# Filter results of the spectral layer stored to memory unit by unit and read back with classes on partitions

## The chip, the cores and the metric

The kernel runs on one core of a Trainium2 chip. A core has a matrix engine (TensorE; its matmuls are PE, its weight loads PEld), a vector engine (DVE), a scalar engine (ACT), GpSimd (POOL) and a queue engine for transfers (SP). They run in parallel, each through its own instructions in order, and wait for each other by semaphores; 16 DMA engines move data between memory and the on-chip buffer of 128 partitions. PSUM, the matmuls' output memory, has eight banks of 512 f32 a partition. The metric is device time in microseconds of the whole program, the median of several runs.

## The reference

Two attention layers and two spectral layers alternate on one sequence of 2048 rows and 1024 columns, f32. In the spectral layer the normalised rows go through a two-dimensional real FFT, are multiplied by a complex filter and come back:

```
def _B_ref(x, w_r, w_i):
    X = jnp.fft.rfft2(x, axes=(-2, -1))
    X = X * (w_r + 1j * w_i)
    return jnp.fft.irfft2(X, s=(S, D), axes=(-2, -1))

x = x + _A_ref(_layernorm(x), A_wqkv, A_wo)
x = x + _B_ref(_layernorm(x), B_w_r, B_w_i)
x = x + _A_ref(_layernorm(x), A_wqkv, A_wo)
x = x + _B_ref(_layernorm(x), B_w_r, B_w_i)
```

## The kernel before

`attention()` and `spectral()` run once for each of two layers. Two buffers of 128 x 16384 f32 hold a whole sequence each: `big` and `R`. `spectral()` has three parts.

*First part.* The transform over one factor of the columns: transposes (`t1`, L1017) and matmuls (`fa`, L1032) put the data into `big`, laid out by g (2 halves), class c (128), q (64).

*Unit loop.* The 256 classes are handled in 32 units (16 of g = 0, then 16 of g = 1), 30 of four frequencies and two of five. `fb(i)` and `fc(i-1)` are the forward matmuls (L1099, L1131), DVE and POOL multiply by the filter `w` (L1138 to L1150; `w` loaded by SP in `loadw`, L1066, 256 KB a unit, two units ahead), `binv(i-3)` and `cinv(i-4)` are the inverse (L1099, L1171). `cinv` ends in an ACT copy (L1177) from PSUM into `big`, in the place of the unit's input. Every second unit SP loads 512 KB of y, the attention result, into `R` (16 loads).

*Last stage.* The inverse over the columns needs the classes on partitions, and in `big` they lie along the row. For each i of 16 and each g, `t2` transposes four 128 x 128 f32 blocks on TensorE (L1207) and ACT copies them to `tt` (L1209). `ai` multiplies them with the constant `mi` (L1219, f32, two passes each), and the results of the two halves are added to y: ACT copies the first (`e`, L1228), DVE takes the difference (L1229) and adds both to the left half of the columns (L1230, L1231), POOL adds the difference to the right half, for two i at a time (L1236; L1233 for i = 14); i = 15 is done on DVE alone (L1242). The transposes of i stand ahead of the matmuls of i - 1.

In layer 0 the last stage also prepares weights of layer 1's attention: `prep` loads staging tiles `wst` (L302), ACT scales them to f16 (L215) and DVE takes the rest (L216), in turns with the stage's work (`next(nxt)`); DVE starts the statistics of the next norm (L1255, six tiles). Behind it `tile_root` and L158 (DVE), L122 (POOL), L365 (ACT), L371 (PE) begin the next layer. In layer 1 the last stage stores the output: seven stores of 1 MB on SP (L1261), in pieces of 512 bytes, and the last 1 MB in two halves on SP and ACT (L1259).

A scheduler sets the order of each engine's instructions; only the last DVE additions are in an order written out by hand. SP issues its transfers in order, and one that waits holds back all behind it.

## Time and profile before

| | us |
|---|---|
| median of 3 runs (lowest, highest) | 3699.69 (3699.19, 3700.08) |
| the profiled execution | 3698.24 |
| its span, first to last instruction | 3696.4 |
| busy in it: PE, DVE, ACT, POOL | 3638.1, 3132.0, 2935.4, 666.2 |
| layer 0: last inverse matmul starts; last stage's last matmul group starts | 1799.74; 1845.21 |
| layer 0: next layer's first statistics (L158) start | 1850.03 |
| layer 1: last inverse matmul starts; last stage's last matmul group starts | 3636.64; 3681.53 |
| mean granted clock of TensorE | 0.997 |

The page sums up busy times over the whole span. A window row gives busy time and count for PE, PEld, DVE, ACT and POOL, then the granted clock, the mean busy share of the 16 DMA engines and GB/s. A timeline row is start, duration, engine, line, operation, output<-input and shape; in brackets the idle time before it and what ended it. A group row gives busy time and mean duration in ns. A transfer row gives size and median time from issue to landing.

### The profile page before, as it was taken

Reading aid. Unit: us, or ns where it says so; the run is one execution under the profiler, and the core shown is the slowest. Engines: PE = TensorE matmul, PEld = TensorE weight load, DVE = VectorE, ACT = ScalarE, POOL = GpSimd, SP = SyncE. Lnnn points to the kernel's source line nnn. Section 1 sums busy time; section 2 is a strip of 40 time slices with the busy share of each in tenths; the row PEclk is TensorE's granted clock in tenths of the full one; section 3 lists DMA queues with packets and bytes.
Section 4 is the critical chain, followed back from the end, with each engine's and each line's share of the span. In section 5 each row is a group of like instructions: output and inputs, shape, how many; then the busy total and the mean of one; then the engine's idle time right before and its main releaser. Section 6 shows DMA issues by size and latency. Waiting matters only on the chain.

```text
span 3696.4 us, 80677 instructions
## 1 busy us (share of the span) xinstructions
PE 3638.1 (98%) x32919; PEld 1628.6 (44%) x32919; DVE 3132.0 (85%) x3800; ACT 2935.4 (79%) x3653; POOL 666.2 (18%) x798
## 2 busy tenths in 40 slices
PE   8999999999999999999999999999999999999998
PEld 5333433343343333378953334333433433333888
DVE  7799899989998989876768898999899889788754
ACT  5788888888888967758747888888888889676686
POOL 1022112211221110014410111111111111100244
PEclk9999999999999999999999999999999999999999
DMA  6122222222232442143151232323222334321423
GB/s 197 21 53 53 52 53 53 58 47 56 47 63 50 99 112 77 70 155 97 56 165 21 56 58 50 56 49 62 42 53 53 63 57 98 101 78 74 171 84 109
DMA packets 203614, 274.33 MB, mean 74 GB/s; under 512 B 75872, under 2 KB 122592, under 8 KB 202208
## 3 DMA queue, kind: packets, MB, share of 16 engines
q1 hardware_dynamic: 164272, 195.06, 16.6%
q0 software_dynamic: 37632, 73.43, 13.8%
q8 instruction: 260, 4.26, 0.5%
q14 instruction: 122, 1.00, 0.1%
q10 hardware_dynamic: 1328, 0.59, 0.1%
HBM read 149.00 MB, written 118.42 MB: 72 GB/s over the span
## 4 chain that ended last, share of the span: by engine, by line


## 5 line engine op out<-in xcount | busy, mean ns | idle before, releaser
L724 ACT ACTIVATE p<-s,bias 128x1024 f32<-128x1024 f32 x2048 | 2171.0, 1112 | 457.5 <-PE s L720 439.5
L743 DVE TENSOR_TENSOR R<-R,p 128x1024 f32<-128x1024 f32 x896 | 1044.7, 1220 | 69.9 <-ACT p L724 67.6
L743 DVE TENSOR_TENSOR acc<-acc,p 128x1024 f32<-128x1024 f32 x896 | 1044.1, 1220 | 55.9 <-ACT p L724 54.9
L730 PE MATMUL o<-p,R 128*32 128x512 f32 x8192 | 985.0, 598 | 0.0
L411 PE MATMUL x<-big,wqk 128*128 128x512 f16 x2880 | 676.4, 380 | 3.2 <-ACT R L473 1.9
L720 PEld LDWEIGHTS <-R 32*128 32x128 f16 x12288 | 229.4, 92 | 740.5 <-issue 624.8
L411 PEld LDWEIGHTS <-wqk 128*128 128x128 f16 x3072 | 275.8, 98 | 418.8 <-issue 127.6
L730 PEld LDWEIGHTS o<-p,R 128*32 128x32 f32 x8192 | 213.7, 109 | 523.4 <-issue 523.4
L720 PE MATMUL s<-Q,R 32*128 32x512 f16 x6144 | 425.4, 378 | 1.9 <-DVE mqk L445 1.9
L720 PE MATMUL s<-R 32*128 32x512 f16 x6144 | 426.3, 377 | 0.2
L469 PE MATMUL x<-wv,big 128*128 128x256 f16 x2784 | 330.5, 275 | 4.1 <-DVE R L216 2.2
L469 PEld LDWEIGHTS <-big 128*128 128x128 f16 x3072 | 291.0, 98 | 96.6 <-issue 55.9
L532 PE MATMUL x<-big 128*128 128x512 f16 x1008 | 231.9, 380 | 0.0
L749 POOL DMA_DIRECT2D zd<-R x112 | 93.4, 834 | 670.3 <-DMA zd<-R 282.2
L749 POOL DMA_DIRECT2D zd<-acc x112 | 92.5, 826 | 656.4 <-DVE z L759 306.8
L532 PEld LDWEIGHTS <-big 128*128 128x128 f16 x1428 | 134.3, 98 | 164.7 <-issue 28.4
L741 DVE SCALAR_TENSOR_TENSOR R<-p 128x1024 f32<-128x1024 f32 x64 | 75.5, 1222 | 97.3 <-ACT p L724 97.3
L752 POOL DMA_DIRECT2D zd<-zd x112 | 89.5, 799 | 367.3 <-DMA zd<-zd 154.8
L1150 DVE TENSOR_TENSOR H<-G,H 128x512 f16<-128x512 f32 (+1 forms) x68 | 47.4, 697 | 98.7 <-ACT H L1149 98.6
L741 DVE SCALAR_TENSOR_TENSOR acc<-p 128x1024 f32<-128x1024 f32 x64 | 75.8, 1221 | 45.1 <-ACT p L724 45.1
L1092 ACT COPY U<-ps 64x256 f32<-64x256 f32 (+1 forms) x272 | 97.2, 357 | 7.9 <-PE ps L1099 2.6
L1099 PE MATMUL ps<-cbi,H 128*128 128x256 f16 (+1 forms) x792 | 99.0, 273 | 3.5 <-DVE H L1150 2.2
(459 smaller groups left out, 3322.9 us busy)
## 6 DMA issues: line engine op xcount, KB each, us to landing
zd<-R POOLq DMA_DIRECT2D x112, 256.0 KB, 4.1
zd<-acc POOLq DMA_DIRECT2D x112, 256.0 KB, 4.1
wst<-in_wp SPq DMA_DIRECT2D x96, 256.0 KB, 3.4
R<-y SPq DMA_DIRECT2D x32, 512.0 KB, 6.0
w<-in_w SPq DMA_DIRECT2D x60, 256.0 KB, 2.7
zt<-zr SPq DMA_DIRECT2D x224, 64.0 KB, 2.7
od<-ohl SPq DMA_DIRECT2D x56, 256.0 KB, 2.4
big<-od SPq DMA_DIRECT2D x12, 896.0 KB, 6.4
```

Source lines behind the costliest of these rows:

```text
L411: nc.tensor.matmul(ps, a, b, start=i == 0, stop=i == 23)
L469: nc.tensor.matmul(ps[:, j], x[c][:, d, o:o + 128], w[:, n, d], start=i == 0, stop=i == 23)
L532: nc.tensor.matmul(p, a, b, start=start and d == ds[0] and i == 0, stop=stop and d == ds[-1] and i == 2)
L720: nc.tensor.matmul(s[h // 2][:, h % 2], K[g][r, a, kt * 128:kt * 128 + 128], Q[g][r, b, c * 512:c * 512 + 512], start=i == 0, stop=i == 2)
L724: nc.scalar.activation(p, s[hf], AF.Exp, bias=bias[g], scale=SCALE / (SQ * SQ))
L730: nc.tensor.matmul(O[g, c][32 * h:32 * h + 32], V[g][:, kt, 32 * h:32 * h + 32], P[g, c, kt, h // 2][:, h % 2], start=kt == 0, stop=kt == ...
L741: last_add = nc.vector.scalar_tensor_tensor(a, P[g, c, 0, hf], 1e-34, p, op0=ALU.add, op1=ALU.add)
L743: last_add = nc.vector.tensor_add(a, a, p)
L749: nc.gpsimd.dma_start(z, a[32 * j:32 * j + 32].rearrange("p a j n -> p (a j n)"), max_dma_last_dim=2048, **({"accum_op": ALU.add} if j els ...
L752: nc.gpsimd.dma_start(z[0:n], z[n:2 * n], accum_op=ALU.add, max_dma_last_dim=2048)
L1092: nc.scalar.copy(ov[64 * r:64 * r + 64, a0:a0 + m, x], tl[64 * x:64 * x + 64, :m, r])
L1099: nc.tensor.matmul(out, l, r, start=k == 0, stop=k == len(mm_) - 1)
```

## The change

`cinv` copies its result to a small tile `T` (three buffers) instead of `big`, and SP stores it to a table `zt` in memory: 256 KB a unit, 1024 pieces of 256 bytes. `turn(i)` reads the unit back in one transfer into eight partitions, 32 KB each, so that classes come to lie on partitions (`turned`, in `R`). The row order of the constant `mi` follows (`row`), and `mi` is loaded once, in layer 0. y is now loaded into `big`, behind the units whose input has been used, over the whole loop; after each spectral layer `big` and `R` swap names (`swap`).

The last stage has no transposes and no `tt`. A half step `ai(a, g)` is eight matmuls whose stationary operand is read from `turned` with a stride of 256 bytes, into one of four PSUM tiles of two banks. `even(a)` takes g = 0: ACT copies to `e` (128x1024), DVE adds; `odd(a)` takes g = 1: DVE subtracts and adds, POOL adds to the right half. Evens 0 to 3 run first. a = 7 is half as before and half on DVE. In layer 0 four of the weight tiles (k0 and q0 parts of the first phase's `wqk`) are scaled and cast on ACT (L321, L322) and subtracted on POOL (L323) instead of DVE.

```diff
+def row(i, s):
+    return 32 * (i % 16 // 4) + 4 * s + i % 4
...
         for i, (h, l, _) in enumerate(sl):
-            split(nc, h, l, st[i], SW)
+            if self.flag is None and ph in PH0[1:]:
+                nc.scalar.activation(st[i], st[i], AF.Copy, scale=SW)
+                nc.scalar.copy(h, st[i])
+                nc.gpsimd.tensor_tensor(l, st[i], h, op=ALU.subtract)
+            else:
+                split(nc, h, l, st[i], SW)
             load()
...
-        t_ = bu[:, g, i % 16]
+        t_ = p3.tile([128, 8, 64], F32, name="T")
         if n == 4:
             nc.scalar.copy(t_.rearrange("p (r j) q -> p j r q", j=4), pt)
         else:
             for o, v in ((0, pt[:, 0:3, 0]), (5, pt[:, 0:3, 1]), (3, pt[:, 3])):
                 nc.scalar.copy(t_[:, o:o + v.shape[1]], v)
+        nc.sync.dma_start(zt[i].rearrange("s p q -> p s q"), t_)
+
+    def turn(i):
+        g, r0 = UNITS[i][0], row(i, 0)
+        nc.sync.dma_start(turned[r0:r0 + 29:4, g], zt[i])
...
+        if 0 <= i - 5 < 32:
+            turn(i - 5)
         if 0 <= i - 4 < 32:
             cinv(i - 4)
...
         if i % 2 and i < 32:
             t = i // 2
-            nc.sync.dma_start(ap.x[:, t], yd[t * 128:(t + 1) * 128, :])
+            nc.sync.dma_start(rest[:, t], yd[t * 128:(t + 1) * 128, :])
+    turn(31)
...
+    ap.swap()
...
+    def ai(a, g):
+        p = pq.tile([128, 8, 128], F32, name="ai")
+        for q in range(8):
+            nc.tensor.matmul(p[:, q], turned[:, g, :, 8 * a + q], cst["mi"][:, g], start=True, stop=True)
+        return p.rearrange("p q (t u) -> p t u q", u=8)
+
+    def even(a):
+        p = ai(a, 0)
+        e = ap.pp.tile([128, 8, 128], F32, name="e", tag="p")
+        ev = e.rearrange("p q (t u) -> p t u q", u=8)
+        x0 = xo[:, 0, a]
+        h = 8 if a < 7 else 4
+        nc.scalar.copy(e[:, :h], p.rearrange("p t u q -> p q (t u)")[:, :h])
+        nc.vector.tensor_add(x0[:, :, :, :h], x0[:, :, :, :h], p[:, :, :, :h])
+        return p, e, ev
+
+    def odd(a, p0, e, ev):
+        p = ai(a, 1)
+        x0, x1 = xo[:, 0, a], xo[:, 1, a]
+        h = 8 if a < 7 else 4
+        nc.vector.tensor_sub(e[:, :h], e[:, :h], p.rearrange("p t u q -> p q (t u)")[:, :h])
+        nc.vector.tensor_add(x0[:, :, :, :h], x0[:, :, :, :h], p[:, :, :, :h])
+        nc.gpsimd.tensor_tensor(x1[:, :, :, :h], x1[:, :, :, :h], ev[:, :, :, :h], op=ALU.add)
...
+    first = [even(a) for a in range(4)]
+    for a in range(8):
+        odd(a, *first.pop(0))
+        if a < 4:
+            first.append(even(a + 4))
```

TensorE, from the last inverse matmuls of layer 0 (L1171) into its last stage. Before:

```order
L1171 MATMUL ps<-ci,U 128x128 x3
L1207 MATMUL ps<-ident,big 128x128 x14
L1219 MATMUL ps<-mi,tt 128x128 x8
L1207 MATMUL ps<-ident,big 128x128 x8
L1219 MATMUL ps<-mi,tt 128x128 x8
```

After (the lines have moved: L1192 is the inverse matmul; each `ai` tile is one half step, in the order even 0 to 3, odd 0, even 4, odd 1, even 5):

```order
L1192 MATMUL ps_21611<-ci_18686,U_21596 128x128 x4
L1238 MATMUL ai_21665<-mi_66,R_93 128x128 x8
L1238 MATMUL ai_21677<-mi_66,R_93 128x128 x8
L1238 MATMUL ai_21689<-mi_66,R_93 128x128 x8
L1238 MATMUL ai_21701<-mi_66,R_93 128x128 x8
L1238 MATMUL ai_21713<-mi_66,R_93 128x128 x8
L1238 MATMUL ai_21725<-mi_66,R_93 128x128 x8
L1238 MATMUL ai_21748<-mi_66,R_93 128x128 x8
L1238 MATMUL ai_21760<-mi_66,R_93 128x128 x8
```

The transposes are gone, and the matmuls read the buffer that the turns fill.

SP at the end of layer 0's loop, where before only filter loads, the constant and then staging loads stood. After (`zt<-T` is the store of a unit, L1206 the turns; the three of L1202 ahead of the last turns are units 28 to 30):

```order
L1206 DMA R<-zt 8x8192 [waits DMAHW7_49,DMAHW4_49]
L1202 DMA zt<-T 128x8x64 [waits DMAHW0_49,Activation_49]
L1202 DMA zt<-T 128x8x64 [waits DMAHW1_49,Activation_49]
L1202 DMA zt<-T 128x8x64 [waits DMAHW2_49,Activation_49]
L1206 DMA R<-zt 8x8192 [waits DMAHW0_49,DMASW1_49]
L1206 DMA R<-zt 8x8192 [waits DMAHW1_49]
L1206 DMA R<-zt 8x8192 [waits DMAHW5_49,DMAHW2_49]
L1202 DMA zt<-T 128x8x64 [waits DMAHW6_49,Activation_49]
L312 DMA wst<-in_wp 128x512 [waits DMAHW7_49,DVE_49,Pool_49]
L312 DMA wst<-in_wp 128x512 [waits PE_49]
L312 DMA wst<-in_wp 128x512
L1206 DMA R<-zt 8x8192 [waits DMAHW6_49]
```

The store of unit 31 now stands behind the turn of unit 30, which waits for that unit's store to land; the turn of unit 31 comes after three staging loads. In layer 1 the same rows stand there without the staging loads.

ACT at the start of layer 0's last stage. Before:

```order
L1209 COPY tt<-ps 128x512 x4
L215 ACTIVATE wv<-wst 128x4x128
L1228 COPY e<-ps 128x512
L215 ACTIVATE wv<-wst 128x4x128 x2
L1209 COPY tt<-ps 128x512 x2
L1228 COPY e<-ps 128x512
```

After, from the copies of units 29 to 31 on:

```order
L1198 COPY T<-ps 128x4x2x64 x3
L1247 COPY e<-ai 128x1024 x4
L218 ACTIVATE wv<-wst 128x4x128 x4
L321 ACTIVATE wst<-wst 128x512
L322 CAST wqk<-wst 128x512
L321 ACTIVATE wst<-wst 128x512
L322 CAST wqk<-wst 128x512
L321 ACTIVATE wst<-wst 128x512
L322 CAST wqk<-wst 128x512
L1247 COPY e<-ai 128x1024
```

The four scalings of `wv` and the first three of `wqk` stand between the copies of `e` for a = 3 and for a = 4. DVE follows the same order after the change:

```order
L1248 TENSOR_TENSOR big<-big,ai 128x16x8x8 x4
L219 SCALAR_TENSOR_TENSOR wv<-wst,wv 128x4x128 x4
L1255 TENSOR_TENSOR e<-e,ai 128x1024
L1256 TENSOR_TENSOR big<-big,ai 128x16x8x8
L1248 TENSOR_TENSOR big<-big,ai 128x16x8x8
L1255 TENSOR_TENSOR e<-e,ai 128x1024
```

Four additions of the evens, four weight splits, then difference and addition of a = 0 and the addition of even 4; before, one split stood between the three DVE operations of each i.

124 lines of the change are left out of this document (52 added, 72 removed).

## The prediction

> **What bounds the kernel now.** The chain that ended last is empty on this page, so the argument goes by the page's first part, then by windows, groups, the timeline and the transfers.
>
> ```profile
> span 3696.4 us, 80677 instructions
> PE 3638.1 (98%) x32919; PEld 1628.6 (44%) x32919; DVE 3132.0 (85%) x3800; ACT 2935.4 (79%) x3653; POOL 666.2 (18%) x798
> ```
>
> TensorE is busy 98% over the span; does that hold where the change works? The windows (busy time of PE, PEld, DVE, ACT, POOL, then clock, DMA share, GB/s) answer by stage: two from the unit loop, the last stage of layer 0, the same stage of layer 1, and the drain behind it.
>
> ```profile
> 1640.00:1700.00 60.00, 56.38 (x509) 50.38 (x508) 38.03 (x91) 46.83 (x115) 24.41 (x34) 1.00 0.57 198
> 1750.00:1800.00 50.00, 49.06 (x436) 45.19 (x435) 29.05 (x66) 44.91 (x114) 21.97 (x31) 1.00 0.20 55
> 1800.00:1850.00 50.00, 48.21 (x388) 47.67 (x387) 41.23 (x63) 32.04 (x57) 22.66 (x8) 1.00 0.18 55
> 3640.00:3680.00 40.00, 40.00 (x327) 40.00 (x327) 24.65 (x39) 24.16 (x42) 18.49 (x6) 1.00 0.47 134
> 3685.00:3690.00 5.00, 0.26 (x3) 0.07 (x1) 2.82 (x9) 0.00 (x0) 1.15 (x1) 0.88 0.90 246
> ```
>
> Loop and last stage are TensorE's (98%, 96%, 100%), and DMA has room in the loop (share 0.20). In the last stage weight loads (PEld) are as busy as the matmuls. After 3685 TensorE is done and only the output drains. So passes taken off the last stage should pay at once, unless DVE (41 of 50 us there), POOL or the output is next.
>
> **The last stage.** The groups of 1800 to 1849 and five rows of the timeline (start, duration) give its pace:
>
> ```profile
> L1219 PEld LDWEIGHTS ps<-mi,tt 128*128 128x128 f32 x256 | 30.3, 194 | 0.5 <-ACT tt L1209 0.5
> L1236 POOL TENSOR_TENSOR R<-R,sd 128x1024 f32<-128x1024 f32 x7 | 21.2, 3030 | 32.3 <-DVE sd L1229 32.3
> L1207 PEld LDWEIGHTS ps<-ident,big 128*128 128x128 f32 x126 | 19.7, 253 | 0.6 <-ACT big L1177 0.6
> ...
> 1808.98 1.90 PEld L1219 LDWEIGHTS ps<-mi,tt 128*128 128x128 f32 x16
> 1809.12 1.95 PE L1219 MATMUL ps<-mi,tt 128*128 128x128 f32 x16
> 1809.71 3.82 DVE L216 SCALAR_TENSOR_TENSOR wv<-wst,wv 128x512 f16<-128x512 f32 x2
> 1810.80 1.25 PEld L1207 LDWEIGHTS ps<-ident,big 128*128 128x128 f32 x8
> 1812.08 1.95 PE L1219 MATMUL ps<-mi,tt 128*128 128x128 f32 x16
> ```
>
> One step i takes 1812.08 − 1809.12 = 2.96 us, 16 of them 47 us: 8 transposes (8 loads, 1.25 us) and 8 matmuls (each f32 matmul is two passes, x16, 1.90 us). The change drops all 128 transposes. But its matmuls load their stationary with a stride of 256 bytes, as the transposes did (253 ns a load against 194 ns for the matmuls' contiguous `tt`). Bounds of 16 passes (one half step `ai(a,g)`): 1.90 us if stride costs nothing, 16 × 1.25/8 = 2.50 us at the transposes' pace. The step leaves 2.96 − 1.90 = 1.06 us net for 8 transposes, which would be 2.1. I take 2.37, nearest the transposes' own row. 16 half steps make 38 us instead of 47: up to **9 us a layer** on TensorE. What is next decides how much of it arrives.
>
> **Layer 0.** The stage ends in a seam:
>
> ```profile
> 1799.74 0.94 PE L1171 MATMUL ps<-ci,U 128*128 128x128 f32 x6
> ...
> 1845.21 3.74 PE L1219 MATMUL ps<-mi,tt 128*128 128x128 f32 x32
> ...
> 1848.47 1.53 POOL L1233 TENSOR_TENSOR R<-R,sd 128x512 f32<-128x512 f32 x1
> 1850.03 0.69 DVE L158 BATCH_NORM_STATS2 fst<-R 128x6 f32<-128x512 f32 x1 [0.69 <-POOL R L1233]
> ```
>
> The next layer starts with L158, which waited for POOL's last addition, so the gain is read at L158. Durations for the new rows: DVE on 128x1024 costs 1.2 us, an ACT copy of that size 1.1 us; splits on ACT 0.65, on DVE 0.69; a weight load lands 2.9 us after issue.
>
> ```profile
> L724 ACT ACTIVATE p<-s,bias 128x1024 f32<-128x1024 f32 x2048 | 2171.0, 1112 | 457.5 <-PE s L720 439.5
> L743 DVE TENSOR_TENSOR R<-R,p 128x1024 f32<-128x1024 f32 x896 | 1044.7, 1220 | 69.9 <-ACT p L724 67.6
> ...
> L215 ACT ACTIVATE wv<-wst 128x512 f16<-128x512 f32 x4 | 2.5, 656 | 0.3 <-DMA wst<-in_wp 0.3
> L1255 DVE BATCH_NORM_STATS2 fst<-R 128x6 f32<-128x512 f32 x6 | 4.0, 686 | 2.5 <-POOL R L1236 2.5
> ...
> L302 SPq DMA_DIRECT2D wst<-in_wp x11: 327/328/717, 1798.2 to 1823.8; - x11
> ...
> DMA to landing us min/median/max: 2.6/2.9/4.5
> ```
>
> Following the new order (the listing of DVE and ACT above): the four evens run 1800.7 to 1810.2 (4 × 2.37), the copy of e3 ends 1811.3. Only then does ACT scale wv: first 1812.0, first split 1812.7. The fourth staging load waits for a buffer that this split frees: lands 1815.9, scaled 1816.6, split 1817.3. The load of q0 waits for that buffer: lands 1820.3, two ACT operations to 1821.6; the copy of e4 stands **behind** them on ACT: 1822.7; the add of even 4 ends 1823.9. Behind it on DVE wait sub and add of a = 1 to 6 (14.4), two evens (2.4), the halves of a = 7 (1.8) and six statistics (4.1): 22.7 us, to 1846.6; POOL's last half addition ends near 1847.4. Against 1850.03: **−2.6 us**. Nothing hides the 11 us in which DVE stands mostly still for staging. The two DVE splits that took 3.82 us together beside POOL's L1236 (0.69 each alone) go to POOL for k0 and q0; as DVE then waits anyway, I count nothing. If loads land at 2.6 and POOL does not slow the splits, −5; if at 4.5, 0.
>
> The Trainium skill, SBUF — State Buffer, "SBUF: two separate sides", has DVE and GpSimd share a port; the 3.82 us agrees, and by it POOL's share of the splits would slow DVE's additions instead: still within these ends.
>
> **Layer 1.** Here the end is output:
>
> ```profile
> 3636.64 0.94 PE L1171 MATMUL ps<-ci,U 128*128 128x128 f32 x6
> ...
> 3681.53 3.74 PE L1219 MATMUL ps<-mi,tt 128*128 128x128 f32 x32
> ...
> q1 hardware_dynamic: 10334, 5.25, 61.7%
> ...
> out<-R SPq DMA_DIRECT2D x7, 1024.0 KB, 5.2
> w<-in_w SPq DMA_DIRECT2D x60, 256.0 KB, 2.7
> zd<-R POOLq DMA_DIRECT2D x112, 256.0 KB, 4.1
> ...
> DMA  0000000897059905990399219930995099999300
> ```
>
> From 3655 to 3685 the 10334 output packets of 512 bytes took 61.7% of 16 engines: 30 × 16 × 0.617/10334 = 28.7 ns each, 3.67 us per MB (2048 packets on 16 engines). The evens run 3637.6 to 3647.1. odd 0 needs the last turn. On SP the write of T(31) stands behind turn(30), which waits for the write of T(30). T(30) is copied by 3637.8; three us (between the 2.7 and 4.1 of the rows above, for 256 KB) for its write, as much for T(31)'s, then 2.7 to 4.1 for turn(31): odd 0 starts 3648 to 3650, I take **3649.0**, a new wait of 2 us on TensorE. Then seven half steps until odd 3 is done (16.6), DVE 1.2, POOL 3.03, issue 0.4, start-up 1.5 (5.2 landing less 3.67), and five MB one behind the other (18.4): +41.1. Before, packets stopped near 3693.0 (the share of DMA in 40 slices of 1.425 us from 3640 on, last row) and the span ended 3.4 us later; so the end is 3649.0 + 44.5 = 3693.5 against 3696.4: **−2.9 us**. Without the output as limit, TensorE would end 8 us earlier; that part is lost to 1 MB stores that now come 2.4 to 3 us apart and take 3.67.
>
> **The loop.** TensorE's order is the same there. Added per unit: a 256 KB write in 256-byte pieces, a 256 KB read into 8 rows, and the reload of y (512 KB every second unit), which before ran at the loop's start (DMA share 0.57 there).
>
> ```profile
> 1662.94 0.59 ACT L1177 COPY big<-ps 128x512 f32<-128x512 f32 x1
> ...
> 1752.67 0.59 ACT L1177 COPY big<-ps 128x512 f32<-128x512 f32 x1
> 1756.76 0.59 ACT L1177 COPY big<-ps 128x512 f32<-128x512 f32 x1
> ...
> 1797.69 0.59 ACT L1177 COPY big<-ps 128x512 f32<-128x512 f32 x1
> ...
> q1 hardware_dynamic: 1728, 3.28, 19.3%
> ...
> q1 hardware_dynamic: 3600, 10.75, 76.2%
> ...
> q1 hardware_dynamic: 7700, 1.91, 65.2%
> ...
> POOL w L1078 <- DMA w<-in_w: 27.7, 15, 3.7
> ```
>
> From the copy of unit 1 to that of unit 29 pass 134.8 us, 4.8 a unit; the fastest are 4.09 apart, some 15 a layer 4.1 to 4.4. Packet costs: w alone (1690 to 1750), 2 KB, 0.193 × 16 × 60/1728 = 107 ns; w and y (1643 to 1683) took 488 us, less 1152 packets of w, over 2448 packets of 4 KB: 149 ns; pieces of 248 bytes (1871 to 1884) 17.6 ns. Per unit and engine: w 8 × 107 = 0.86; y 4 × 149 = 0.60; the write 64 pieces at 17.6 to 28.7 ns = 1.13 to 1.84; the turn 0.60 if spread over 16 engines, 1.19 if only 8 take part (256 KB in 32 rows landed in 4.1 us, in 128 rows in 2.7). Together 3.2 to 4.5 us. I take 3.8: it fits under 4.09, covered by TensorE; w may land some us later (POOL already waits for it off the path). **0 us**; uncovered it is the slow rival. Moving y away from the start may return a part of the 3.6 us that TensorE idles in 1640 to 1700: −1 to 0, counted 0.
>
> The Trainium skill, DMA: Bandwidth & Descriptors, "Why a DMA increments its semaphore by 16 and not by 1", speaks against this change: the engines used are the largest number up to 16 that divides the slowest dimension, which gives a turn 8, the lowest-numbered; no run here shows it yet, and by it the busy eight would have 3.8 to 4.5 us of work a unit. The same page's Specifications call pieces under 512 bytes a read-modify-write; by that the write would stand at its upper end or over it, while the 17.6 ns of the 248-byte rows (which are not such writes) does not show it.
>
> **Sum.** −2.6 − 2.9 + 0 = −5.5 on the profiled execution of 3698.24: 3692.7. The median is 1.45 higher, so 3694.2.
>
> **Rivals.**
> - *Stride is free, or cover is better* (faster). Half steps of 1.90 us: layer 0's evens end 1.9 earlier and the staging chain with them (−4.5), layer 1's odd 3 comes 7 × 0.47 = 3.3 earlier and odd 0 at 3648 (−7): −11.5, so 3688. For: 1.06 us net for 8 transposes. Against: 253 to 194 ns on PEld.
> - *DMA bounds the loop* (slower). The place is the w load behind writes and turns on the same engines; the price is what exceeds the unit. With the write at 28.7 ns a piece the 15 fastest units lose 0.4 each: +12 in two layers, less 5.5, 3706. From 35 ns on (2.2 + 2.65 of the others) the load passes the mean unit of 4.8 and all pay: at 40 ns 5.2, 0.4 × 31 × 2 = +25, less 5.5, 3719. I give it 3706 to 3719, 3712 in the middle; it decides from about 30 ns a piece on. For: no row of before writes pieces of 256 bytes to memory, and the turn has few rows. Against: share 0.20 now.
> - *The ends eat it* (no gain): the turn(31) wait and staging both at their long ends, 3650 + 44.5 and 1850: −2 or up to +4, inside no change.
>
> **Chances.** Forecast (3692 to 3699) 0.42; stride free or better cover 0.30; DMA-bound loop 0.23; ends 0.05. About 0.2%, 7.4 us, is what a measurement of this kernel can tell from no change: the forecast lies inside it, the first rival outside, the second mostly outside above (0.01 of it, and the ends, are no change). Faster 0.30, same 0.48, slower 0.22. The likeliest case alone spans 3690 to 3699; with most of both rivals, 3685 to 3714.
>
> **What would show it.** Half steps: spacing of the new matmul rows at 2.4, not 1.9. Loop: units still 4.1 to 4.4 apart, TensorE's share 98%, DMA share near 0.7; if PE waits for w products, the slow rival holds. Layer 0: idle DVE between 1812 and 1823 in front of splits, L161 near 1847. Layer 1: odd 0 two us after even 3, outputs back to back. Wrong if the write of a unit lands much later than 4 us, since each turn and, in layer 1, the end hang on two such writes in a row.

## The result, and the profile after

The changed kernel takes 3838.05 us (median of four runs, 3835.76 to 3842.95) beside 3699.44 us for the kernel before, measured beside it: a ratio of 1.0377, interval 1.0359 to 1.0395. It is 139 us slower, and the prediction (3694.2, range 3685 to 3714) was wrong in sign and size. First the totals of the page of the changed kernel, then the same stages as windows (busy PE, PEld, DVE, ACT, POOL, then granted clock, DMA share, GB/s): two of the unit loop, the last stage of layer 0 and that of layer 1.

```profile
span 3834.0 us, 80120 instructions
PE 3681.4 (96%) x32663; PEld 1653.3 (43%) x32663; DVE 3120.2 (81%) x3754; ACT 2901.5 (76%) x3579; POOL 663.4 (17%) x802
```

```profile
1640.00:1700.00 60.00, 54.24 (x497) 48.70 (x495) 34.62 (x80) 45.92 (x113) 21.17 (x30) 1.00 0.54 150
1750.00:1800.00 50.00, 35.42 (x288) 30.44 (x287) 19.38 (x44) 28.96 (x77) 15.37 (x23) 0.97 0.54 150
1850.00:1900.00 50.00, 47.45 (x228) 46.41 (x227) 21.19 (x22) 19.17 (x31) 16.09 (x10) 0.99 0.37 107
3780.00:3820.00 40.00, 40.00 (x184) 40.00 (x183) 21.89 (x20) 4.12 (x5) 17.86 (x7) 1.00 0.47 131
```

There are 256 matmul records fewer, yet PE is busy 43 us longer, and in the loop (1750 to 1800) it now stands idle for 14.6 of 50 us where it idled 0.9. DMA is busy 0.54 of that time, so it is not full. In the last stage of layer 1 TensorE is busy all the time, as before. Four rows of the timeline split the loss (the last two inverse matmul groups, the next layer's first statistics, the output stage's matmuls):

```profile
1856.15 0.94 PE L1192 MATMUL ps<-ci,U 128*128 128x128 f32 x6 [0.28 <-ACT U L1113]
1916.46 0.69 DVE L161 BATCH_NORM_STATS2 fst<-big 128x6 f32<-128x512 f32 x1 [0.59 <-POOL big L1257]
3764.46 0.94 PE L1192 MATMUL ps<-ci,U 128*128 128x128 f32 x6 [0.28 <-ACT U L1113]
3765.23 56.38 PE L1238 MATMUL ai<-mi,big 128*128 128x128 f32 x256
```

| stretch | before, us | after, us | difference |
|---|---|---|---|
| start to the last inverse group of layer 0 | 1799.74 | 1856.15 | +56.4 |
| from there to the next layer's statistics | 50.29 | 60.31 | +10.0 |
| from there to the last inverse group of layer 1 | 1786.61 | 1848.00 | +61.4 |
| from there to the end of the span | 59.76 | 69.54 | +9.8 |

The four add up to 137.6 us, the difference of the two spans (3834.0 − 3696.4). So 118 us arise ahead of the last inverse groups of the two layers, nearly all of it in the unit loops (the first filter product of layer 0 starts at 1649.62 before and 1650.54 after; from the next layer's statistics to the first product of layer 1 it is 1638.05 and 1638.67 us), which the prediction had at 0, and 20 us in the last stages, which it had at −5.5.

**What TensorE waits for in the loop.** The waits of the changed kernel from 1700 to 1800 (who waits for whom, us in all, times, longest):

```profile
DVE H L1171 <- ACT H L1170: 57.7, 16, 5.1
PEld L1120 <- ACT H L1170: 30.3, 16, 2.8
ACT U L1113 <- PE ps L1120: 28.5, 14, 3.2
PE ps L1120 <- ACT H L1170: 27.3, 14, 2.6
```

No transfer is among them. TensorE (L1120, `binv`) and DVE (L1171, the low half of `H`) wait for ACT's cast of `G` to `H` (L1170), and ACT waits for TensorE. Why the cast is late stands in the order of ACT. In the loop of layer 0 before the change (L1092 copies the results of `fb`, B, and of `binv`, U; L1149 is the cast; numbers of tiles grow in the order of the program, in which `fc(i-1)`, which makes H, stands behind `fb(i)`, which makes B):

```order
L1092 COPY B_20818<-ps_20805 64x2x128 x4
L1092 COPY U_20856<-ps_20843 64x2x128 x3
L1149 CAST H_20824<-G_20823 128x2x256
L1092 COPY U_20856<-ps_20843 64x2x128
L1177 COPY big_87<-ps_20861 128x4x2x64
L1092 COPY B_20880<-ps_20867 64x2x128 x4
```

The same place after the change (L1113 are the copies, L1170 the cast, L1198 the copies to `T`):

```order
L1113 COPY B_20015<-ps_20002 64x2x128 x4
L1113 COPY U_20052<-ps_20039 64x2x128 x4
L1113 COPY B_20079<-ps_20066 64x2x128 x4
L1170 CAST H_19952<-G_19951 128x2x256
L1113 COPY U_20120<-ps_20107 64x2x128 x4
L1113 COPY B_20148<-ps_20135 64x2x128 x4
L1198 COPY T_20063<-ps_20058 128x4x2x64
L1170 CAST H_20021<-G_20020 128x2x256
```

Before, the cast of unit j came behind the B copies of unit j + 1 (20824 behind 20818). Now it comes behind those of unit j + 3 (20021 belongs to the unit ahead of B_20015, and B_20079 and B_20148 are passed first). TensorE runs `fb(j + 3)`, `binv(j)`, `fb(j + 4)`, `binv(j + 1)`. So the cast of j + 1 waits on ACT behind the copies of `fb(j + 4)`, this stands on TensorE behind `binv(j)`, and `binv(j)` needs the cast of j: a closed circle. The timeline shows one turn of it:

```profile
1796.32 0.63 ACT L1170 CAST H<-G 128x512 f16<-128x512 f32 x1
...
1797.00 0.39 PE L1120 MATMUL ps<-cbi,H 128*128 128x256 f16 x2 [2.37 <-ACT H L1170]
...
1797.23 0.39 PE L1192 MATMUL ps<-ci,U 128*128 128x128 f32 x2
...
1799.50 1.47 PE L1120 MATMUL ps<-cb,big 128*128 128x256 f16 x12
...
1799.94 0.72 POOL L1167 TENSOR_TENSOR G<-G,t__21017 128x256 f32<-128x256 f32 x1
...
1801.07 1.50 ACT L1113 COPY B<-ps 64x256 f32<-64x256 f32 x4 [0.48 <-PE ps L1120]
1802.59 0.62 ACT L1170 CAST H<-G 128x512 f16<-128x512 f32 x1
```

Cast, `binv`, `fb` of the next unit, its copies, cast: 6.27 us in this turn. In the turn before it (its cast starts at 1789.10) two copies to `T` stand in the circle as well, and it takes 7.22; the two kinds alternate, some 6.7 us a unit. The row of 1797.23 shows that TensorE's order changed a little too: two matmuls of `cinv` now stand between the first two of `binv` and its other ten, where before all twelve of `binv` came first. POOL had finished the G that this cast reads at 1800.66 (1799.94 + 0.72); the cast was held to 1802.59 by the copies ahead of it on ACT. The timeline of ACT before has the cast in the middle of the U copies:

```profile
1751.64 0.62 ACT L1149 CAST H<-G 128x512 f16<-128x512 f32 x1
1752.28 0.37 ACT L1092 COPY U<-ps 64x256 f32<-64x256 f32 x1
1752.67 0.59 ACT L1177 COPY big<-ps 128x512 f32<-128x512 f32 x1
1753.15 1.51 ACT L1092 COPY B<-ps 64x256 f32<-64x256 f32 x4
...
1755.73 0.62 ACT L1149 CAST H<-G 128x512 f16<-128x512 f32 x1
```

4.09 us a unit, and no idle time in front of these rows.

**The last stages.** By the source line of the new matmuls (duration in ns min/median/max):

```profile
L1238 PEld LDWEIGHTS ai<-mi,big x256: 295/313/314, 3765.1 to 3821.1; 128*128 128x128 f32 x128
L1238 PE MATMUL ai<-mi,big x256: 378/383/384, 3765.2 to 3821.2; 128*128 128x128 f32 x128
```

A load takes 313 ns where the contiguous `tt` took 194 and the strided transposes 253. 16 half steps last 56.38 us, 3.52 each, not 2.37.

### The profile page after: what moved, and what is told of

It reads as the page before. It is cut to its first block, busy times and chain, and to the rows that moved or that the text cites. A ratio compares the mean times of both kernels' runs of the same rounds, so it can differ in the third digit from the quotient of the medians.

```text
span 3834.0 us, 80120 instructions
## 1 busy us (share of the span) xinstructions
PE 3681.4 (96%) x32663; PEld 1653.3 (43%) x32663; DVE 3120.2 (81%) x3754; ACT 2901.5 (76%) x3579; POOL 663.4 (17%) x802
## 4 chain that ended last, share of the span: by engine, by line
## 5 line engine op out<-in xcount | busy, mean ns | idle before, releaser
L759 DVE TENSOR_TENSOR big<-big,p 128x1024 f32<-128x1024 f32 x448 | 522.4, 1219 | 38.4 <-ACT p L740 37.1
L759 DVE TENSOR_TENSOR R<-R,p 128x1024 f32<-128x1024 f32 x448 | 522.1, 1219 | 31.4 <-ACT p L740 30.1
L746 PE MATMUL o<-p,R 128*32 128x512 f32 x4096 | 492.5, 598 | 0.0
L746 PE MATMUL o<-p,big 128*32 128x512 f32 x4096 | 492.5, 598 | 0.0
L426 PE MATMUL x<-R,wqk 128*128 128x512 f16 x1440 | 338.1, 380 | 1.9 <-ACT big L488 1.2
L426 PE MATMUL x<-big,wqk 128*128 128x512 f16 x1440 | 338.2, 380 | 1.4 <-ACT R L488 0.7
L1171 DVE TENSOR_TENSOR H<-G,H 128x512 f16<-128x512 f32 (+1 forms) x68 | 45.5, 671 | 231.2 <-ACT H L1170 231.2
L736 PE MATMUL s<-R 32*128 32x512 f16 x3072 | 213.6, 377 | 0.1
L736 PE MATMUL s<-Q,big 32*128 32x512 f16 x3072 | 212.7, 377 | 1.0 <-DVE mqk L460 1.0
L736 PE MATMUL s<-Q,R 32*128 32x512 f16 x3072 | 212.6, 378 | 1.0 <-DVE mqk L460 1.0
L736 PE MATMUL s<-big 32*128 32x512 f16 x3072 | 212.4, 377 | 0.1
L1120 PE MATMUL ps<-cbi,H 128*128 128x256 f16 (+1 forms) x792 | 116.0, 288 | 98.7 <-ACT H L1170 92.5
L1113 ACT COPY U<-ps 64x256 f32<-64x256 f32 (+1 forms) x272 | 97.2, 357 | 110.9 <-PE ps L1120 108.0
```

The costliest lines, as they stand in the source:

```text
L426: nc.tensor.matmul(ps, a, b, start=i == 0, stop=i == 23)
L736: nc.tensor.matmul(s[h // 2][:, h % 2], K[g][r, a, kt * 128:kt * 128 + 128], Q[g][r, b, c * 512:c * 512 + 512], start=i == 0, stop=i == 2)
L746: nc.tensor.matmul(O[g, c][32 * h:32 * h + 32], V[g][:, kt, 32 * h:32 * h + 32], P[g, c, kt, h // 2][:, h % 2], start=kt == 0, stop=kt == ...
L759: last_add = nc.vector.tensor_add(a, a, p)
L1113: nc.scalar.copy(ov[64 * r:64 * r + 64, a0:a0 + m, x], tl[64 * x:64 * x + 64, :m, r])
L1120: nc.tensor.matmul(out, l, r, start=k == 0, stop=k == len(mm_) - 1)
```

## The experiments

The readings so far are of one trace each. They leave two theories for the loop: the order on ACT makes it slow, or the added transfers do and the order only shows it. For the last stages the stride of the stationary operand stands against the other work beside it. All runs (one execution each, the median of four where an interval is given), against the kernel before measured beside them:

| run | us | over the kernel before | ratio, interval |
|---|---|---|---|
| the changed kernel | 3838.05 | +138.6 | 1.0377, 1.0359 to 1.0395 |
| e1_turn_later | 3819.40 | +122.2 | |
| e2_before_late_cast | 3821.65 | +124.5 | |
| e3_no_transfers | 3714.28 | +17.1 | |
| e4_strides | 3852.68 | +155.5 | |
| e5_order_by_hand | 3756.27 | +57.9 | 1.0156, 1.0139 to 1.0173 |
| e6_order_and_contiguous | 3727.24 | +28.8 | |
| e7_before_strided_tt | 3757.39 | +59.0 | |
| e8_reads_only | 3815.06 | +116.7 | |
| e9_sp_order_too | 3768.48 | +69.4 | 1.0188, 1.0171 to 1.0205 |
| e10_compact_first | 3758.57 | +59.5 | 1.0164, 1.0147 to 1.0181 |
| e11_hand_no_transfers | 3729.49 | +30.3 | |
| e12_filter_earlier | 3776.33 | +77.1 | 1.0208, 1.0191 to 1.0225 |
| e13_pairs_16_rows | 3763.34 | +64.2 | 1.0173, 1.0156 to 1.0190 |
| e14_readback_later | 3739.06 | +40.6 | 1.0109, 1.0092 to 1.0126 |
| e15_readback_and_filter | 3741.59 | +43.2 | 1.0115, 1.0099 to 1.0132 |

### Which of the two makes the loop slow

**e1**, the changed kernel with its read-backs three units later:

```diff
-        if 0 <= i - 5 < 32:
-            turn(i - 5)
+        if 0 <= i - 8 < 32:
+            turn(i - 8)
...
-    turn(31)
+    for i in range(36 - 8, 32):
+        turn(i)
```

> The changed kernel with each unit's read-back put three units further back in the program (turn(i-8) instead of turn(i-5)); all transfers are kept, and the scheduler then sets ACT's cast H of unit j behind the B copies of unit j+1, as in the kernel before, instead of behind those of unit j+3. Theory O (the loop is slow because of the order of ACT and DVE: a chain cast, inverse matmuls, U and B copies, next cast, without overlap): units come back to 4.1 to 4.8 us, and the time falls by about 110 to 120 us, to 3715 to 3730. Theory D (the transfers bound the loop: stores in 256-byte pieces and reads into eight rows hold the filter loads): the bytes are the same, units stay near 6.7 us and the time near 3838.

The premise failed: the order of before did not come back, the cast still stands behind the B copies of unit j + 3, and the loop stayed slow (PE busy 35.83 of the 50 us from 1750). So this run does not tell the theories apart; +122.2 beside +138.6 is all that later read-backs gave here.

**e2**, the kernel before with only products and cast moved; `fc` is cut into matmuls, products and cast, the products come one unit later (as in the changed kernel, where DVE's products of a unit start one `fc` later than before), and the cast of j is tied behind the B copies of j + 3. No transfer is added:

```diff
+        if 0 <= i - 3 < 32:
+            with tc.issue_after(end[i].ins) if i in end else nullcontext():
+                fch(i - 3)
+        if 0 <= i - 2 < 32:
+            fcp(i - 2)
         if 0 <= i - 1 < 32:
-            fc(i - 1)
+            fcm(i - 1)
```

> The kernel before, with no store and no read-back, but with the cast of unit j put behind the B copies of unit j+3 (the products one unit later, the cast tied behind those copies), which is the changed kernel's order on ACT. Theory O: units go from 4.1-4.8 to 6.2-6.9 us and the time from 3699 to about 3800 to 3825, with no transfer added. Theory D: nothing but a few us, below 3710.

The window of its loop, and four rows of ACT's timeline:

```profile
1750.00:1800.00 50.00, 35.53 (x310) 31.40 (x308) 20.22 (x47) 32.98 (x89) 16.54 (x24) 1.00 0.15 43
```

```profile
1772.00 1.50 ACT L1092 COPY B<-ps 64x256 f32<-64x256 f32 x4
1773.52 0.62 ACT L1166 CAST H<-G 128x512 f16<-128x512 f32 x1
...
1778.45 1.50 ACT L1092 COPY B<-ps 64x256 f32<-64x256 f32 x4
1779.97 0.62 ACT L1166 CAST H<-G 128x512 f16<-128x512 f32 x1
```

The order alone costs 124.5 us, with DMA at a share of 0.15: the same circle, 6.45 us a unit, the same 35.5 us of TensorE in 50. That is as much as the 118 us of the changed kernel's loops, and it arises in the loops: the last stages of e2 take 50.3 and 59.5 us, as before. Nor is the clock the cause: it was 0.97 in this window of the changed kernel and 1.00 here.

**e3**, the changed kernel without the stores and read-backs (the `dma_start` lines of L1202 and L1206 become `pass`):

> The changed kernel without the unit stores and without the read-backs (the last stage multiplies whatever lies in the buffer); the scheduler's order is then that of the kernel before. Theory O: like the run with the later read-back within some 5 us, 3715 to 3725, the rest over 3699 being the last stages' slower matmuls. Theory D: also fast, since the transfers are gone; it is the difference to the run with the later read-back that shows what the transfers cost: under O below 5 us, under D 100 us or more.

```profile
1750.00:1800.00 50.00, 49.27 (x439) 45.82 (x436) 28.16 (x64) 45.34 (x114) 21.57 (x31) 1.00 0.37 117
```

Without them the scheduler writes the order of before (the cast of j between the U copies behind B of j + 1), and TensorE is full again. What is left, +17.1 us, are the last stages, whose half steps still read the strided buffer: they take 59.5 and 69.6 us, 9.2 and 9.8 more than before, while the stretches ahead of them are each some 1.5 us shorter.

**e8**, the changed kernel without the stores; each read-back takes y in its place (8 rows of 32 KB), so that it waits for no store:

```diff
-        nc.sync.dma_start(zt[i].rearrange("s p q -> p s q"), t_)
+        pass
...
-        nc.sync.dma_start(turned[r0:r0 + 29:4, g], zt[i])
+        yr = yd[64 * i:64 * i + 64, :].rearrange("(a b) d -> a (b d)", b=8)
+        nc.sync.dma_start(turned[r0:r0 + 29:4, g].rearrange("p n q -> p (n q)"), yr)
```

> The changed kernel without the unit stores; each read-back takes the same 256 KB in eight rows of 32 KB, from y instead of the table, so it waits for no store (the last stage multiplies other numbers). The scheduler still puts the cast of unit j behind the B copies of unit j+3. Theory O: the loop stays slow, 6.2 to 7 us a unit, 3805 to 3840. Theory W (SP waits at each read-back for the store to land and so holds the filter loads): fast, 3714 to 3725, since nothing waits for a store. Theory D: in between, as a quarter of the loop's bytes is gone.

```profile
1750.00:1800.00 50.00, 38.05 (x322) 33.20 (x322) 21.61 (x48) 31.95 (x82) 16.79 (x24) 1.00 0.39 124
```

Still slow, still with the late cast, although no small piece goes to memory and nothing waits for one. The cost of the stores is not the cause. What in the added read-backs makes the scheduler hold the cast back was not found. They are enough for it without stores (e8), a distance up to i − 8 does not help (e1), and the copies to `T`, which e3 keeps, do not bring it about; stores without read-backs were not run.

### The order mended, and what is left in the loop

**e5**, the changed kernel with the order of PE, ACT, DVE and POOL in the loop written out, the cast right behind the U copies of `binv` (SP still by the scheduler):

```diff
+    eng = mybir.EngineType
+    with tc.manual_schedule(engines={eng.Activation, eng.DVE, eng.PE, eng.Pool}):
...
+            if 0 <= i - 3 < 32:
+                binv(i - 3)
+            cast()
+            if 0 <= i - 5 < 32:
+                turn(i - 5)
```

> The changed kernel with all its transfers, where the loop's instructions on TensorE, ACT, DVE and GpSimd stand in the order of the kernel before, by hand: per unit forward matmuls, products, inverse matmuls and U copies, then the cast H of unit j between the B copies of units j+1 and j+2; SP's order is still the scheduler's. (In the run with the later read-back the order had not come back: there the cast still stood behind the B copies of unit j+3.) Theory O (order): units of 4.1 to 4.8 us, TensorE 97% busy in the loop, 3714 to 3725, some 115 us under the changed kernel and 15 to 25 over the one before. Theory D (transfers): the loop is held by filter loads and stores, units over 6 us, 3800 or more; then POOL or DVE wait for the filter, not for each other.

80.7 us (138.6 − 57.9) come back, but the expected 3714 to 3725 is missed: TensorE is busy 46.61 of the 50 us from 1750, and units come in pairs of some 10.3 us. Its longest wait of that window is new:

```profile
POOL w L1099 <- DMA w<-in_w: 24.2, 10, 4.2
```

Every second `w` load on SP stands behind a store, a read-back and a load of y.

**e9**, e5 with SP's order written out too: `w`, read-back, store, y. I thought that this would free `w`:

```diff
-    with tc.manual_schedule(engines={eng.Activation, eng.DVE, eng.PE, eng.Pool}):
+    with tc.manual_schedule(engines={eng.Activation, eng.DVE, eng.PE, eng.Pool, eng.SP}):
```

> As the run with the order by hand, and SP's transfers by hand too: per unit the filter load for two units on first, then the read-back of the unit before, the store, and every second unit y; all bytes and all sizes are unchanged. In the run with only the compute order by hand every second filter load stood on SP behind a store, a read-back and y, and units came in pairs of 10.3 us. Theory S (SP's order held the filter loads): 4.1 to 4.8 us a unit, about 40 us faster than that run, 3712 to 3722, equal to the run without transfers (3714). Theory D (the DMA engines themselves are the limit, 64% busy on average, more on the eight that serve a read-back): little change, 3745 to 3757, POOL still waiting for the filter some 30 to 40 us in 100.

It did not: 12 us slower than e5. SP's own timeline suggests why (start and duration of the issue):

```profile
1752.08 0.38 SPq L1205 DMA_DIRECT2D zt<-T  x1
...
1756.34 0.63 SPq L1209 DMA_DIRECT2D R<-zt  x1
1757.06 0.39 SPq L1205 DMA_DIRECT2D zt<-T  x1
...
1761.42 0.63 SPq L1209 DMA_DIRECT2D R<-zt  x1
1762.15 0.39 SPq L1205 DMA_DIRECT2D zt<-T  x1
```

A store is issued; 4.3 us later the read-back of the same unit can go; only then the next store. SP takes 5.0 to 5.2 us a round where TensorE needs 4.1, and everything behind it, `w` too, runs at that pace. Two edits followed from two theories: `w` is asked for too late (e12), or SP itself is held by the store that it has just issued (e14).

**e11**, the control: e9 without stores and read-backs.

> Control for the run with SP by hand: the same order by hand on all engines, without the unit stores and read-backs (the last stage multiplies what lies in the buffer); filter loads and y stay. If the hand order itself is as good as the scheduler's in the kernel before: 3712 to 3720, units of 4.1 to 4.4, as in the run without transfers (3714), and the 50 us over it in the run with SP by hand are what the transfers cost. If the hand order is worse: 3740 to 3770, and the transfers cost little.

+30.3 us, between the two expectations. Against e3's +17.1 the order by hand costs 13 us, so the transfers cost 39 of e9's 69. Some 25 of these arise ahead of the last inverse groups and 14 in the last stages, which take 67.0 and 76.5 us in e9 and 59.5 and 69.6 in e11: SP is behind with the read-backs there.

**e12**, e9 with `w` three units ahead in a third buffer, and its sign product and maximum a unit later:

```diff
-        loadw(i + 2)
+        loadw(i + 3)
+        signs(i + 1)
```

> As the run with SP by hand, all transfers kept, but the filter is loaded three units ahead instead of two (a third buffer), and POOL's sign product on it and DVE's maximum stand one unit later, so that a load may take a unit longer before anything waits. Theory L (the transfers cost only because a filter load now takes some 5 us instead of 2.7 to land and POOL, in order, waits for it): 3712 to 3725, units of 4.1 to 4.6. Theory B (the DMA engines, or the eight that serve a read-back, are full: 4.2 us of work or more a unit): units stay at 4.8 to 5.1, 3740 to 3768.

No gain over e9 (+77.1 beside +69.4), although TensorE is busy 49.72 of 50 us from 1750. Only the place of the loss moved: SP's rounds are still about 5 us or longer, it falls behind, and the backlog is paid at the end, where the last copy to `T` waits 4.33 us for a store. The filter loads were not the limit; the time lies above the range of the other theory too.

**e13**, e12 with two units read back by one transfer into 16 neighbouring partitions:

```diff
-    return 32 * (i % 16 // 4) + 4 * s + i % 4
+    return 8 * (i % 16) + s
...
-        g, r0 = UNITS[i][0], row(i, 0)
-        nc.sync.dma_start(turned[r0:r0 + 29:4, g], zt[i])
+        if i % 2:
+            g, r0 = UNITS[i][0], row(i - 1, 0)
+            nc.sync.dma_start(turned[r0:r0 + 16, g], zt[i - 1:i + 1].rearrange("u s p q -> (u s) p q"))
```

> As the run with the filter earlier, but two units are read back by one transfer into 16 neighbouring partitions (the rows of the constant follow), so twice as many rows take part in each. Theory E (eight rows keep only eight of the 16 DMA engines busy): where the run before is still held by the DMA engines, 15 to 40 us faster; where it already runs at 4.1 to 4.6 us a unit, within 5 us of it. If rows do not matter: within 5 us in either case.

13 us better than e12, between the two expectations, yet the transfers from 1740 to 1790 (packets, MB, share of 16 engines) got slower, first e12, then e13:

```profile
q1 hardware_dynamic: 11951, 10.09, 70.4%
```

```profile
q1 hardware_dynamic: 13556, 10.75, 98.8%
```

7% more bytes take 40% more of the engines' time. The pairs also halve the number of waits on SP, so what the 13 us come from is not settled.

**e14**, e9 with the read-back two units later, so that SP need not wait for the store it has just issued; **e15**, e12 with the same:

```diff
-            if 0 <= i - 5 < 32:
-                turn(i - 5)
+            if 0 <= i - 7 < 32:
+                turn(i - 7)
...
-    turn(31)
+    for i in range(29, 32):
+        turn(i)
```

> As the run with SP by hand, but each unit is read back two units later (turn(i-7)), so that the store it needs was issued three units before instead of one; bytes, sizes and the order of all else are the same. In the run with SP by hand the queue went round in 5.0 to 5.2 us: a store, some 4.2 us until it had landed and the read-back's wait ended, the read-back's issue, the next store. Theory C (that chain on SP holds the loop): the loop comes back to the control without transfers (its last unit copy in layer 0 at 1804 us, against 1818), 25 to 40 us faster than 3768, 3728 to 3743. Theory B (the DMA engines are full): within 8 us of 3768.

> The same two units' delay of the read-back on the run with the filter earlier (three buffers, sign product one unit later). Theory C: also 25 to 45 us faster than that run (3776), 3731 to 3750; where filter loads still land late, this one is the faster of the two by up to 10 us. Theory B: within 8 us of 3776.

e14 gives −29.4 us against e9, e15 −34.7 against e12 (medians), both as expected. The last copy to `T` of layer 0 comes 9.5 us earlier than in e9, first e9, then e14:

```profile
1818.32 0.58 ACT L1201 COPY T<-ps 128x512 f32<-128x512 f32 x1 [2.74 <-DMA zt<-T]
```

```profile
1808.84 0.58 ACT L1201 COPY T<-ps 128x512 f32<-128x512 f32 x1 [0.46 <-PE ps L1195]
```

It no longer waits for a store, and stands 4.9 us behind the control e11 (1803.97); the last stages are back at the control's 59.5 and 69.7 us. So most of what the transfers cost in e9, 29 of 39 us, was SP, held by a read-back whose store was still on its way. The other 10 us stand in the two loops, and their cause is open. `w` a unit earlier adds nothing on top (e15 is 2.5 us behind e14, with overlapping intervals).

### The last stages

**e4**, the changed kernel with the stationary read at one stride for each a, 64, 32, 16, 8, 4, 2, 1 and 64 floats (the same amount of work):

```diff
-            nc.tensor.matmul(p[:, q], turned[:, g, :, 8 * a + q], cst["mi"][:, g], start=True, stop=True)
+            w = (64, 32, 16, 8, 4, 2, 1, 64)[a]
+            st = 128 * w * (8 * a + q) % 8192 if w < 64 else 8 * a + q
+            nc.tensor.matmul(p[:, q], flat[:, g, st:st + 127 * w + 1:w], cst["mi"][:, g], start=True, stop=True)
```

> The changed kernel with the stationary operand of the last stage read at other strides: 256 bytes for a=0 and 7, then 128, 64, 32, 16, 8 and 4 bytes (contiguous) for a=1 to 6; it multiplies other columns than it should. The weight loads of the f32 matmuls took 313 ns at 256 bytes against 192 ns contiguous in the kernel before. If any stride costs: half steps of 3.5 us for all a but 6, and 1.9 us for a=6 (where nothing else bounds them). If it is a matter of how far apart the elements lie: 3.5 us falls step by step, with 1.9 us from some stride under 64 bytes on. If the layout has nothing to do with it (two passes of a matmul in this position): 3.5 us for all.

The first DVE or ACT row behind each half step starts when it is done, so the differences are the half steps of a = 4, 1, 5, 2 and 6:

```profile
3802.11 1.22 DVE L1259 TENSOR_TENSOR e<-e,ai 128x1024 f32<-128x1024 f32 x1 [1.25 <-PE ai L1242]
...
3805.85 1.01 ACT L1251 COPY e<-ai 128x1024 f32<-128x1024 f32 x1 [6.24 <-PE ai L1242]
...
3809.37 1.22 DVE L1259 TENSOR_TENSOR e<-e,ai 128x1024 f32<-128x1024 f32 x1 [1.25 <-PE ai L1242]
...
3811.25 1.01 ACT L1251 COPY e<-ai 128x1024 f32<-128x1024 f32 x1 [4.39 <-PE ai L1242]
...
3814.74 1.22 DVE L1259 TENSOR_TENSOR e<-e,ai 128x1024 f32<-128x1024 f32 x1 [1.22 <-PE ai L1242]
...
3816.52 1.01 ACT L1251 COPY e<-ai 128x1024 f32<-128x1024 f32 x1 [4.26 <-PE ai L1242]
```

16 bytes 3.74 us, 128 bytes 3.52, 8 bytes 1.88, 64 bytes 3.49, 4 bytes 1.78. The price does not grow with the stride: it is there in full from 16 bytes on and gone at 8. (That the whole run is slower than the changed kernel is another matter: before even 1 TensorE stands still for 9.8 us in layer 1, until 4.1 us after the issue of the last read-back.)

**e7** puts the same price into the kernel before: `tt` is stored so that a block's columns lie 16 bytes apart, with equal values.

```diff
-        tt = ap.pp.tile([128, 4, 128], F32, name="tt", tag="p")
-        nc.scalar.copy(tt, pt)
+        tt = ap.pp.tile([128, 128, 4], F32, name="tt", tag="p")
+        nc.scalar.copy(tt.rearrange("p c j -> p j c"), pt)
```

> The kernel before with the transposed blocks stored so that the second matmul reads its stationary operand with a stride of 16 bytes instead of contiguously; the values are the same. If f32 matmuls with a strided stationary operand pay on their own: the 16 passes per step go from 1.90 us to 3.4 to 3.8 us, 16 steps and two layers, +48 to +60 us, 3745 to 3760 (a little more if ACT's copy with strided writes becomes slow). If the cost belongs to the changed kernel's buffer alone: no change, 3697 to 3701.

The groups of its layer 0 stage (1810 to 1850):

```profile
L1219 PE MATMUL ps<-mi,tt 128*128 128x128 f32 x134 | 32.6, 396 | 0.0
L1219 PEld LDWEIGHTS ps<-mi,tt 128*128 128x128 f32 x135 | 32.4, 330 | 0.0
L1209 ACT COPY tt<-ps 128x512 f32<-128x512 f32 x16 | 16.7, 1159 | 11.9 <-PE ps L1207 11.9
```

330 ns a load instead of 194: 256 loads a layer × 136 ns = 35 us, of which 29.5 a layer arrive in the time (+59.0). ACT's copies, which now write the stride, take 1159 ns, but ACT waits for TensorE, so it is the loads that count.

**e6**, e5 with the stationary contiguous:

```diff
-            nc.tensor.matmul(p[:, q], turned[:, g, :, 8 * a + q], cst["mi"][:, g], start=True, stop=True)
+            st = 128 * (8 * a + q)
+            nc.tensor.matmul(p[:, q], flat[:, g, st:st + 128], cst["mi"][:, g], start=True, stop=True)
```

> The same order by hand, and the last stage's stationary operand read contiguously (128 columns in a row instead of every 64th, so it multiplies other numbers than it should). The run with several strides showed half steps of 3.4 to 3.8 us at 16 bytes and above, 1.8 to 1.9 us at 8 and 4. If stride is the whole loss of the last stages, half steps take 1.9 us and the time falls by another 20 to 28 us against the run with order alone, to 3688 to 3700, at or under the kernel before; if something else bounds those stages, by less than 8.

The groups of its last stages, first layer 0 (1800 to 1900), then layer 1 from odd 0 on (3683 to 3712):

```profile
L1248 PE MATMUL ai<-mi,R 128*128 128x128 f32 x256 | 31.5, 290 | 6.3 <-DMA R<-zt 6.3
...
L1248 PE MATMUL ai<-mi,big 128*128 128x128 f32 x192 | 23.9, 292 | 6.0 <-issue 6.0
L1248 PEld LDWEIGHTS ai<-mi,big 128*128 128x128 f32 x192 | 23.7, 208 | 6.2 <-issue 6.2
```

−29.0 us against e5, a little more than expected of the edit; the absolute time does not hold, since e5 itself lay 31 us above the upper end of its own. Half steps take 1.8 to 2.0 us, and in each layer a wait of 6 us for the last read-back, which the slow matmuls had covered, comes to light. Even so the last stages, 45.9 and 56.6 us, are 4.4 and 3.2 shorter than before the change. That is the gain that the change was after, but e6 has it only with other columns than the layer needs.

**e10** makes the operand contiguous with the values kept: ACT copies each half step's 128x1024 to a tile ahead of e9's matmuls.

```diff
+            tts.append(ap.pp.tile([128, 8, 128], F32, name="tt", tag="p"))
+            nc.scalar.copy(tts[-1], turned[:, g, :, 8 * a:8 * a + 8].rearrange("p n q -> p q n"))
...
-            nc.tensor.matmul(p[:, q], turned[:, g, :, 8 * a + q], cst["mi"][:, g], start=True, stop=True)
+            nc.tensor.matmul(p[:, q], tt[:, q], cst["mi"][:, g], start=True, stop=True)
```

> As the run with SP by hand, and in the last stage ACT copies each half step's columns into a contiguous tile (128x1024, two half steps ahead) before the matmuls read it; the output is the reference's. If the stride of the stationary operand is the loss of the last stages, half steps go from 3.5 to 1.9-2.3 us where ACT keeps up (it has 16 more copies of 1.1 us a layer): 20 to 28 us under the run with SP by hand. Under theory S that is 3688 to 3702, about the kernel before or just under it; under theory D 3720 to 3735.

Only −9.9 us against e9. In layer 0 (1825 to 1890):

```profile
L1255 PE MATMUL ai<-mi,tt 128*128 128x128 f32 x210 | 30.3, 311 | 16.8 <-ACT tt L1248 16.8
...
L1248 ACT COPY tt<-R 128x1024 f32<-128x1024 f32 x13 | 25.4, 1999 | 8.0 <-issue 8.0
```

The stride's price moved to ACT: a copy that reads at 256 bytes takes 2.0 us, not the 1.1 counted on (the copies of that size to `e`, out of PSUM, take 1.0), and TensorE waits for it. No kernel of this study beats the kernel before; the best with all of the change's work is e14, 1.1% slower.

## Why the prediction was wrong, point by point

- **"The loop. TensorE's order is the same there", "0 us".** This step failed, with 118 of the 138 us. TensorE's groups did keep their order, but for two matmuls of `cinv` a unit, and the step asked only for the price of the transfers. It took the order of ACT and DVE in the loop for unchanged; the orders it had looked at were those of the last stages and of SP. A cast two units later closes a circle of 6.3 to 7.2 us a unit where 4.1 were needed, and e2 shows that this order costs as much with no transfer added; e3, that without the transfers the scheduler does not write it.
- **"I take 2.37, nearest the transposes' own row".** This step failed too, as a term mis-sized: 3.52 us a half step, outside the bounds 1.90 to 2.50, so the last stages came out at +10.0 and +9.8 instead of −2.6 and −2.9. The bound was taken from another kind of load: the transposes' 253 ns belong to another operation, and the matmuls' strided loads take 313 (the changed kernel) to 330 (e7). Why the transposes' loads, at the same stride of 256 bytes, take less was not tried.
- **Rival "DMA bounds the loop" (3706 to 3719).** The side was right, the mechanism was not: with the order mended, transfers cost 39 us in e9 and some 10 in e14. The 29 between them are SP's wait for a store to land, not the engines' load (DMA share 0.54 in the changed kernel's slow loop, 0.71 in e9's, 0.76 in the faster e14's). Its place, "the w load behind writes and turns", was seen in e5, on SP's queue.
- **Rival "stride is free".** Excluded by the same rows, and by more than was thought. What it would have been worth is seen in e6: 4.4 us in layer 0, as it said (4.5), and 3.2 instead of 7 in layer 1, where TensorE then waits 6 us for the last read-back.
- **The ends.** The stores and turns behind the last unit of layer 1 came in the order worked out, but the last turn was issued at 3774.5, 8.4 us behind the last copy to `T` (3766.1), where two writes of three us had been counted. (The terms named there give 3646.5 to 3647.9 for odd 0, not the 3648 to 3650 written, so the wait of 2 us was under 1 by its own figures.) It cost nothing: the four evens now last 14 us, and TensorE had no wait before odd 0. In e6, where it had one, the turn took 4.1 us from issue (3678.89) to odd 0 (3683.04). "Outputs back to back" did not come before the fifth store of 1 MB: the first five are two half steps, 7.0 us, apart and take 3.7, and TensorE is the limit.
- **The write's price.** Bounded at 17.6 to 28.7 ns a piece of 256 bytes; from the runs it can only be estimated. The 107 and 149 ns are means over packets that include 16 small ones a transfer; a whole load of `w` takes 15.4 us of engine time (twelve in 185 us, 1690 to 1750 before the change) and one of y 21.8, which makes 0.96 and 0.68 us a unit and engine, not 0.86 and 0.60. In e9's loop (1740 to 1790) ten of `w`, five of y, ten turns and ten stores took 571 us. With a turn at 9.5 us (64 × 149 ns) some 21 ns a piece are left for the stores; with a turn at 15 us, as e8's 331 us for eight of `w`, four of y and eight turns give it, 15. The Trainium skill (DMA: Bandwidth & Descriptors, Specifications) calls such pieces a read-modify-write; either estimate lies under the 28.7 ns of the 512-byte pieces, so no surcharge over those shows here. The same page's rule on the eight engines of a turn was never tried alone: e13 has 16 rows, but fewer waits as well.

The sum closes as follows, in us over the kernel before: 138.6 (the change), 69.4 with the order by hand (e9; 57.9 with SP's by the scheduler, e5), 40.6 with the read-back later (e14), 30.3 without transfers (e11), 17.1 without transfers and with the scheduler's own order (e3). What remains there stands in the last stages and goes with the strided loads: e6 takes 29 us off e5 by making them contiguous. Not settled: why the scheduler moves the cast, what the hand-written order loses (13 us), and what e14 still pays for transfers (10 us).

## What to carry to other kernels

When a change adds instructions to a scheduled loop, compare the new order with the old on **every** engine of that loop, above all where a producer of the bound engine sits, and look for a circle that closes through two engines' orders; an unchanged order on the bound engine proves little. A layout that saves transposes is only free if the matmul can read it: price the strided operand by its own row or a small run before the rest is built on it. A transfer that waits for another's landing belongs far enough behind it in its queue that the queue never stops.

## What the runs showed of the hardware

- A load of an f32 stationary of 128x128 at a stride of 16 bytes or more took 313 to 330 ns (the changed kernel, e4, e7), at 8 bytes or less 192 to 208 (e4, e6); a half step of eight such matmuls 3.5 to 3.7 us against 1.8 to 1.9. Between 16 and 256 bytes the stride hardly mattered.
- ACT pays for strides too: 1159 ns instead of about 600 for 128x512 written at 16 bytes (e7), 2.0 us for 128x1024 read at 256 bytes, where one of that size out of PSUM took 1.0 (e10).
- A read-back into 16 neighbouring partitions raised the engines' busy share from 70.4% to 98.8% at 7% more bytes (e13); its cause was not tried.
- A read-back could be issued 4.3 us after the store ahead of it on SP (e9), and a round of 5.0 to 5.2 us on SP set the pace of a loop that needs 4.1; with two units between store and read-back 29 us came back (e14).
